# Fused attention and feed-forward: keys loaded straight with two heads side by side, three key and query buffers, values loaded later, key operands made in three portions

## The chip, the cores and the metric

The kernel runs on one core of a Trainium2 chip. The metric is the device time of one execution in microseconds; the profile gives the span from the first to the last instruction of one execution, and some time lies around it. The engines are named as in the profile: PE is TensorE (PEld its weight loads), DVE is VectorE, ACT is ScalarE, POOL is GpSimd, SP is SyncE, whose queue issues every DMA of this kernel.

## The reference

Block-compressed local attention over 2 batches of 8 heads (768 positions, 64 columns), then a feed-forward layer and a second one with a softmax-weighted norm. Cut to what matters:

```python
k_sum = k.reshape(B, H, nb, block, D).max(axis=3)      # block = 32
v_sum = v.reshape(B, H, nb, block, D).mean(axis=3)
scores_l = scale * (q @ k.T)                           # kept where |i - j| < 16
scores_s = scale * (q @ k_sum.T) + np.log(block)
a = softmax(concat([scores_l masked, scores_s]))
attn = a @ concat([v, v_sum])
x = attn heads side by side, 1536 x 512
h = x @ w_in;  y = (h * np.cos(h)) @ w_out             # 512 -> 2048 -> 512
h2 = y @ w_in2; solu = h2 * softmax(h2)                # 512 -> 1024
out = (layernorm(solu) * g_ln) @ w_out2                # 1024 -> 512
```

The weights come as 64-bit floats, read as pairs of 32-bit words.

## The kernel before

Attention comes first. Two heads make a pair (`n`, 0 to 7), and 4 tiles of 64 queries of a pair make a group (`G`, 0 to 23, three to a pair). A hand-written loop runs over `step` (0 to 28) and puts the stages of different groups behind each other: at a step, `emit_s` forms the scores of group step + 1 (`sps`), `emit_max` adds the mask and takes the row maximum of group step (VectorE, four instructions, then a subtraction on GpSimd), `emit_exp` takes the exponentials of group step - 1 (ScalarE), `emit_sum` and `emit_norm` the row sums (VectorE) and the normalisation (GpSimd) of group step - 2, `emit_t` and `emit_at` transpose the probabilities of group step - 4 on TensorE (`aps`) and copy them out (`at`, ScalarE, from group 20 on VectorE), and `emit_av` and `emit_x` form the products with the values of group step - 5 (`ops`) and copy them to `X`. Every engine takes its instructions in the order in which the code issues them.

Per pair, the keys and queries are loaded (`load_k`, `load_q`), copied so that the two heads lie side by side (`pair_k`, `pair_q`, tiles `kg` and `qg`), transposed on TensorE into the PSUM tile `qk` (`emit_k`, `emit_q`, at the step with g = 2, two pairs ahead), reduced to block maxima (`emit_ksum`, VectorE) and copied by ScalarE into the operands of the scores: `kx` in three instructions (inner windows, end windows, block maxima) and `qx`. The values are loaded in overlapping windows of 96 rows (`load_v`); `sum_v` sums them by blocks on TensorE, `scale_v` turns the sums into means on ScalarE (`vm`), and `place_vsum` writes the means with two DMAs into rows 96 to 119 of the value tile `vt`, from which the value products read them. `VSUM_AT` says at which step each pair's sums are formed; the means are placed one step later.

Beside this, the first eight weight tiles of the feed-forward are converted (`Weights`): `WSTEPS` lists the steps at which a tile is taken up (`bits`, which also issues the load of the next); ScalarE rescales its two words a step later, VectorE joins them (`s`), and the step after, ScalarE rounds the result (`w`) and GpSimd takes the difference. From step 15 on `fill` puts three or four products of the first feed-forward tiles (`h`) into each step. `warm_up` issues products of a zero tile.

SyncE's queue issues loads in the order of the code and stands still at an instruction whose buffer or semaphore is not free. By their shapes a load of keys or queries of a pair moves 384 KB, one of values 576 KB in four DMAs, a weight tile (`raw`) 512 KB, the means of a pair 144 KB in two DMAs, the mask 360 KB, the identity 64 KB.

From step 24 on the first feed-forward steps (`drain`) are mixed in; the feed-forward proper follows.

Of the kernel before, what the change touches and what calls it, by code (L numbers as in the profile page):

```python
# [18 lines left out]
BLOCK = 32  # L19
# [15 lines left out]
def fused_kernel(  # L35
# [58 lines left out]
    WSTEPS = (3, 6, 9, 12, 15, 18, 19, 20)  # L94
# [240 lines left out]
    def attention():  # L335
        st = ExitStack()
        with st:
# [27 lines left out]
            def load_k(n):  # L365
                k_t[n] = load_heads(k, n, "kt", 2)

            def side_by_side(t, name, scalar):
# [3 lines left out]
                if scalar:  # L372
                    nc.scalar.activation(out=to, in_=t, func=AF.Copy)
                else:
                    nc.vector.tensor_copy(to, t)
# [64 lines left out]
            def transposed(t, even, odd):  # L440

                for c in range(S // P):
                    nc.tensor.transpose(
                        (even, odd)[c % 2][:, (c // 2) * P:(c // 2 + 1) * P],
                        t[:, c].rearrange("p h d -> p (h d)"), ident)

            def emit_k(n):
                qk = ps_qk.tile([P, 2, 2, S // 2], F32, tag="qk", name="qk")
                transposed(k_t.pop(n), qk[:, 0, 0], qk[:, 0, 1])
                qk_t["k", n] = qk[:, 0]  # L450
                qk_t["q", n] = qk[:, 1, 0], qk[:, 1, 1]

            def emit_ksum(n):
                ksum = io.tile([P, NS], F32, tag="ksum", name="ksum")
                nc.vector.tensor_reduce(
                    out=ksum, in_=strided(qk_t["k", n], 0, [[BLOCK // 2, NS], [S // 2, 2], [1, BLOCK // 2]]),
                    op=ALU.max, axis=AX.XY)
                ks_t[n] = ksum

            def emit_kx(n):  # L460
                kps = qk_t.pop(("k", n))
                kx = io.tile([P, NT, KW], F32, tag="kx", name="kx")
                win = kx[:, :, 0:WIN].rearrange("p t (i r) -> p t r i", r=2)
# [8 lines left out]
                kx_t[n] = kx  # L472
# [10 lines left out]
            def emit_qx(n):  # L483
# [11 lines left out]
                kx_t[n] = (qx, kx_t[n])  # L495
# [3 lines left out]
            def emit_s(G):  # L499
                n, g = divmod(G, GPP)  # L500
                qx, kx = kx_t[n]
# [90 lines left out]
            warm_up(7)  # L592
            pair_k(0)
            emit_k(0)
            emit_ksum(0)
            pair_q(0)
            emit_q(0)
            emit_kx(0)
            emit_qx(0)
# [6 lines left out]
            VSUM_AT = {1: 0, 2: 1, **{3 * m - 2: m for m in range(2, NPAIR)}}  # L606
            for step in range(NGR + LA):
                n, g = divmod(step, GPP)
                summed = LN <= step < NGR + LN
                ahead = n + 1 if g == 0 and n + 1 < NPAIR else 0  # L610
# [4 lines left out]
                if step == 0:  # L615
                    emit_max(0)
                    pair_k(1)
# [19 lines left out]
                if ahead and step:  # L637
# [4 lines left out]
                if ahead and not step:  # L642
# [9 lines left out]
                if ahead:  # L652
                    emit_kx(ahead)
                    emit_qx(ahead)
# [7 lines left out]
                if g == 1 and n + 2 < NPAIR:  # L662
                    pair_k(n + 2)
# [5 lines left out]
                if g == 1 and n + 2 < NPAIR:  # L669
                    load_v(n + 2)  # L670
# [307 lines left out]
```

## Time and profile before

| | us |
|---|---|
| median of 3 runs | 492.09 (491.07 to 492.64) |
| the profiled execution: time | 493.62 |
| the profiled execution: span | 491.8 |
| TensorE busy (share of the span) | 477.3 (97%) |
| VectorE busy | 294.7 (60%) |
| ScalarE busy | 313.7 (64%) |
| GpSimd busy | 147.0 (30%) |

A busy TensorE is not one at its peak, and shares over the whole span are means over stages with different limits: attention takes the first fifth, where the transfers and all engines are in use, and the feed-forward the rest, in which TensorE hardly stops. The granted clock is 0.999 of full over the span.

### The profile page before, as it was taken

To read this page: it belongs to the slowest core of one execution; us is meant where nothing else is said; L and a number is where in the kernel's file an instruction comes from. 1 tells how busy PE (TensorE), PEld (TensorE's weight loads), DVE (VectorE), ACT (ScalarE), POOL (GpSimd) and SP (SyncE) were. 2 spreads that over 40 slices of the span, in tenths; PEclk is the share of its full clock that TensorE was granted. 3 is DMA by queue.
4 is the path that set the end of the run, shared out by engine and by line. 5 is a ranking of instruction groups with operands and counts; after the bars stand their busy time and mean duration, and the time that the engine had idled before them with its cause. 6 is when DMAs were issued, how large, how long until landed. Compare 5 with 4: busy or idle time off the path is not lost.

```text
span 491.8 us, 7868 instructions
## 1 busy us (share of the span) xinstructions
PE 477.3 (97%) x2938; PEld 391.7 (80%) x2938; DVE 294.7 (60%) x667; ACT 313.7 (64%) x540; POOL 147.0 (30%) x144
## 2 busy tenths in 40 slices
PE   7889999999999999999999999999999999999997
PEld 4677787678888888888888888888888888888886
DVE  3656775783445446556474655556477766776661
ACT  2568878756686666556655653788624867777621
POOL 1467887822432223222222220245500011110000
PEclk9999999999999999999999999999999999999999
DMA  7988964301222322232223220220001333224211
GB/s 206 239 222 221 258 146 110 110 2 39 91 85 85 116 99 87 87 123 92 85 90 119 92 85 23 93 100 1 0 1 43 87 86 86 66 64 65 68 39 44
DMA packets 59046, 46.17 MB, mean 94 GB/s; under 512 B 40448, under 2 KB 51328, under 8 KB 59008
## 3 DMA queue, kind: packets, MB, share of 16 engines
q1 hardware_dynamic: 59008, 45.67, 32.5%
q8 instruction: 23, 0.38, 0.3%
q14 instruction: 15, 0.12, 0.1%
HBM read 36.61 MB, written 3.15 MB: 81 GB/s over the span
## 4 chain that ended last, share of the span: by engine, by line
PE 84%; ACT 5%; DMA 3%; POOL 3%; issue 1%; SPq 1%; DVE 1%; ACTq 0%
PE y L276 27%; PE h L234 26%; PE o L853 13%; PE h L739 13%; DMA qt<-in_q_dram 2%; PE ops L562 1%; PE aps L544 1%; POOL sm L522 1%; PE sps L507 1%; ACT at L552 1%; DMA raw<-in_moe_w_in_dram 1%; ACT kx L464 1%; POOL w L187 1%; ACT sm L527 1%; SPq L393 1%
## 5 line engine op out<-in xcount | busy, mean ns | idle before, releaser
L234 PE MATMUL h<-xs,w 128*128 128x512 f32 x576 | 141.2, 391 | 0.0
L276 PE MATMUL y<-gs,w 128*128 128x512 f32 x576 | 138.2, 389 | 0.0
L276 PEld LDWEIGHTS y<-gs,w 128*128 128x128 f32 x576 | 108.0, 188 | 22.5
L234 PEld LDWEIGHTS h<-xs,w 128*128 128x128 f32 x576 | 107.2, 188 | 21.6
L187 POOL TENSOR_TENSOR w<-s,w 128x512 fp32r<-128x512 f32 x48 | 62.2, 1296 | 162.6 <-ACT w L186 139.6
L243 ACT ACTIVATE r<-h 128x512 int32<-128x512 f32 x48 | 28.6, 596 | 85.9 <-PE h L234 85.9
L248 DVE SCALAR_TENSOR_TENSOR r<-r,h 128x512 f32<-128x512 int32 x48 | 32.9, 685 | 67.2 <-ACT r L243 67.1
L171 DVE SCALAR_TENSOR_TENSOR s<-raw 128x512 int32<-128x512 int32 x48 | 35.8, 746 | 59.5 <-ACT raw L164 52.1
L853 PE MATMUL o<-w,ls 128*128 128x512 f32 (+1 forms) x312 | 67.8, 373 | 0.0
L739 PE MATMUL h<-w,xs 128*128 128x512 f32 x288 | 67.6, 390 | 0.0
L853 PEld LDWEIGHTS o<-w,ls 128*128 128x128 f32 x312 | 55.3, 188 | 10.7 <-DVE ls L829 0.4
L739 PEld LDWEIGHTS h<-w,xs 128*128 128x128 f32 x288 | 53.9, 188 | 11.2
L204 POOL TENSOR_TENSOR xs<-X,xs 128x512 fp32r<-128x512 f32 x22 | 30.6, 1397 | 39.1 <-ACT xs L203 39.1
L774 POOL TENSOR_TENSOR st<-st,mhalf 128x1 f32<-128x1 f32 x12 | 6.6, 550 | 110.1 <-DVE st L773 91.7
L253 ACT ACTIVATE r<-r,half_pi 128x512 f32<-128x512 f32 x48 | 34.4, 717 | 1.3 <-DVE r L248 1.3
L264 DVE TENSOR_TENSOR gs<-h,gs 128x512 fp32r<-128x512 f32 x48 | 32.6, 679 | 4.2 <-ACT gs L263 4.0
L163 ACT ACTIVATE raw<-raw 128x512 f32<-128x512 f32 x48 | 31.9, 664 | 2.0 <-DMA raw<-in_moe_w_in_dram 2.0
L258 DVE TENSOR_TENSOR h<-h,r 128x512 f32<-128x512 f32 x48 | 32.9, 684 | 0.4 <-ACT r L253 0.4
L164 ACT ACTIVATE raw<-raw 128x512 int32<-128x512 uint32 x48 | 31.9, 664 | 0.0
L186 ACT ACTIVATE w<-s 128x512 fp32r<-128x512 f32 x48 | 30.2, 629 | 1.5 <-DVE s L171 1.1
L756 ACT ACTIVATE e<-h,st 128x1024 f32<-128x1024 f32 (+1 forms) x13 | 13.6, 1048 | 26.4 <-DVE st L752 22.9
L522 POOL TENSOR_TENSOR sm<-sm,mx 128x480 f32<-128x480 f32 x24 | 24.1, 1006 | 17.6 <-DVE mx L518 17.5
(79 smaller groups left out, 553.9 us busy)
## 6 DMA issues: line engine op xcount, KB each, us to landing
raw<-in_moe_w_in_dram SPq DMA_DIRECT2D x24, 512.0 KB
raw<-in_moe_w_out_dram SPq DMA_DIRECT2D x24, 512.0 KB
vt<-in_v_dram SPq DMA_DIRECT2D x16, 240.0 KB
kt<-in_k_dram SPq DMA_DIRECT2D x8, 384.0 KB
qt<-in_q_dram SPq DMA_DIRECT2D x8, 384.0 KB
out_dram<-osb SPq DMA_DIRECT2D x11, 256.0 KB
vt<-vm SPq DMA_DIRECT2D x16, 72.0 KB
vt<-in_v_dram SPq DMA_DIRECT2D x16, 48.0 KB
```

The lines of the kernel that those rows point to most:

```text
L163: nc.scalar.activation(out=hw, in_=hw, func=AF.Prelu, scale=REBIAS, alpha=NEGATIVE)
L164: nc.scalar.activation(out=lw, in_=lw.bitcast(U32), func=AF.Copy, scale=TOP3)
L171: nc.vector.scalar_tensor_tensor(out=self.f32[i], in0=t[:, :, 1], scalar=3, in1=t[:, :, 0], op0=ALU.logical_shift_left, op1=ALU.bitwise_or)
L187: nc.gpsimd.tensor_tensor(out=w[:, 1, :], in0=f, in1=as32(w[:, 0, :]), op=ALU.subtract)
L234: nc.tensor.matmul(h, lhsT=w[:, a, f * P:(f + 1) * P], rhs=xs_of[tb, c][:, b_, :], start=(m == 0), stop=(m == 3 * KC - 1))
L248: nc.vector.scalar_tensor_tensor(out=r, in0=r.bitcast(I32), scalar=TWO_PI, in1=h_of[step], op0=ALU.mult, op1=ALU.subtract)
L253: nc.scalar.activation(out=r, in_=r, func=AF.Sin, scale=-1.0, bias=half_pi)
L258: nc.vector.tensor_tensor(out=h, in0=h, in1=r, op=ALU.mult)
L264: nc.vector.tensor_tensor(out=gs[:, 1, :], in0=r, in1=as32(gs[:, 0, :]), op=ALU.subtract)
L276: nc.tensor.matmul(y[e], lhsT=w[:, a, e * P:(e + 1) * P], rhs=gs[:, b_, :], start=(f == 0 and i == 0), stop=(f == GF - 1 and i == 2))
L739: nc.tensor.matmul(banks[n], lhsT=xs_of[NTB + t // TPB, c][:, a, t0:t0 + P], rhs=weights.done[w2i[c][n]][:, b_, :], start=(m == 0), stop=( ...
L853: nc.tensor.matmul(o, lhsT=ls_of[t][f // 4][:, a, s0:s0 + P], rhs=w[:, b_, cols], start=(f == 0 and i == 0), stop=(f == NF2 - 1 and i == 2))
```

## The change

Keys are loaded by two DMAs, one for each head, in pieces of 64 numbers, straight into the layout with two heads side by side; `pair_k` and the copy `kg` are gone. The transposed keys then stand in their natural order in PSUM, so that `ksum` and `kx` read them without a stride. Key and query tiles have three buffers instead of two. The first queries' copy moves from ScalarE to GpSimd. `kx` is split: the inner windows stay at the step with g = 0, the end windows and block maxima move to g = 1, and `qx` to g = 2 of the pair before. The first values are loaded after the keys and queries of pair 2, the others by a table `VLOAD_AT`; `VSUM_AT` forms the sums later, and `WSTEPS` takes the weight tiles up one step later. There are five more warm-up products.

```diff
-    WSTEPS = (3, 6, 9, 12, 15, 18, 19, 20)
+    WSTEPS = (4, 7, 10, 13, 16, 19, 20, 21)
...
-                t = io.tile([P, 2, NR, D], F32, tag=name, name=name)
+                t = io.tile([P, 2, NR, D], F32, tag=name, name=name, bufs=3)
...
             def load_k(n):
-                k_t[n] = load_heads(k, n, "kt", 2)
+                b, hp = divmod(n, NP)
+                t = k_t[n] = io.tile([P, NR, 2, D], F32, tag="kt", name="kt", bufs=3)
+                for j in range(2):
+                    nc.sync.dma_start(out=t[:, :, j, :], in_=k[b, 2 * hp + j].rearrange("(c p) d -> p c d", p=P))
...
-            def pair_k(n):
-                k_t[n] = side_by_side(k_t[n], "kg", False)
-
             def pair_q(n):
-                q_t[n] = side_by_side(q_t[n], "qg", n < 2)
+                q_t[n] = side_by_side(q_t[n], "qg", (nc.gpsimd, nc.scalar)[n] if n < 2 else nc.vector)
...
             def emit_k(n):
                 qk = ps_qk.tile([P, 2, 2, S // 2], F32, tag="qk", name="qk")
-                transposed(k_t.pop(n), qk[:, 0, 0], qk[:, 0, 1])
-                qk_t["k", n] = qk[:, 0]
+                t = k_t.pop(n)
+                kps = qk_t["k", n] = qk[:, 0].rearrange("p a s -> p (a s)")
+                for c in range(NR):
+                    nc.tensor.transpose(kps[:, c * P:(c + 1) * P], t[:, c].rearrange("p h d -> p (h d)"), ident)
...
             def emit_ksum(n):
                 nc.vector.tensor_reduce(
-                    out=ksum, in_=strided(qk_t["k", n], 0, [[BLOCK // 2, NS], [S // 2, 2], [1, BLOCK // 2]]),
-                    op=ALU.max, axis=AX.XY)
+                    out=ksum, in_=qk_t["k", n].rearrange("p (s b) -> p s b", b=BLOCK), op=ALU.max, axis=AX.X)
...
             def emit_kx(n):
                 nc.scalar.activation(
                     out=win[:, 1:NT - 1],
-                    in_=strided(kps, (QT - BAND) // 2, [[QT // 2, NT - 2], [S // 2, 2], [1, WIN // 2]]), func=AF.Copy)
+                    in_=strided(kps, QT - BAND, [[QT, NT - 2], [1, WIN]]), func=AF.Copy)
+
+            def emit_kx_ends(n):
+                kps, kx = qk_t.pop(("k", n)), kx_t["k", n]
+                win = kx[:, :, 0:WIN]
                 nc.scalar.activation(
                     out=win[:, 0:NT:NT - 1],
-                    in_=strided(kps, 0, [[(S - WIN) // 2, 2], [S // 2, 2], [1, WIN // 2]]), func=AF.Copy)
+                    in_=strided(kps, 0, [[S - WIN, 2], [1, WIN]]), func=AF.Copy)
                 nc.scalar.activation(
                     out=kx[:, :, WIN:KW], in_=ks_t.pop(n).unsqueeze(1).to_broadcast([P, NT, NS]), func=AF.Copy)
...
             load_k(1)
             load_q(1)
-            load_v(0)
             load_k(2)
             load_q(2)
-            load_v(1)
+            load_v(0)
...
-            VSUM_AT = {1: 0, 2: 1, **{3 * m - 2: m for m in range(2, NPAIR)}}
+            VSUM_AT = {3: 0, 4: 1, 7: 2, 9: 3, 12: 4, 13: 5, 16: 6, 19: 7}
+            VLOAD_AT = {1: 1, 4: 2, 6: 3, 8: 4, 10: 5, 13: 6, 16: 7}
...
+                if g == 1 and 0 < n < NPAIR - 1:
+                    emit_kx_ends(n + 1)
...
                 if ahead:
                     emit_kx(ahead)
-                    emit_qx(ahead)
+                if step == 1:
+                    emit_kx_ends(1)
+                if step == 0:
+                    emit_qx(1)
+                if g == 2 and n + 2 < NPAIR:
+                    emit_qx(n + 2)
...
                 if g == 1 and n + 2 < NPAIR:
-                    pair_k(n + 2)
                     pair_q(n + 2)
...
-                if g == 1 and n + 2 < NPAIR:
-                    load_v(n + 2)
+                if step in VLOAD_AT:
+                    load_v(VLOAD_AT[step])
```

How the order of instructions moves is shown at three places. First SyncE's queue at steps 2 to 4, where the block means `vm` of pairs 0 and 1 are written; a number behind a name tells buffers apart. Before, `vt_266` is the values of pair 2, `raw_319` and `raw_353` are weight tiles 0 and 1, `vt_121` the values of pair 0 and `kt_405` the keys of pair 4:

```order
L389 DMA vt_266<-in_v_dram 96x10x64
L393 DMA vt_266<-in_v_dram 96x2x64
L139 DMA raw_319<-in_moe_w_in_dram 128x1024
L436 DMA vt_121<-vm_271 12x12x128 x2
L139 DMA raw_353<-in_moe_w_in_dram 128x1024
L436 DMA vt_130<-vm_323 12x12x128 x2
L357 DMA kt_405<-in_k_dram 128x6x128
L357 DMA qt_407<-in_q_dram 128x2x384
```

Now `raw_292` and `raw_375` are weight tiles 0 and 1, `kt_380` the keys of pair 4, `vt_385` the values of pair 2 and `vt_128` those of pair 0:

```order
L139 DMA raw_292<-in_moe_w_in_dram 128x1024
L139 DMA raw_375<-in_moe_w_in_dram 128x1024
L369 DMA kt_380<-in_k_dram 128x6x64 x2
L357 DMA qt_383<-in_q_dram 128x2x384
L389 DMA vt_385<-in_v_dram 96x10x64
L393 DMA vt_385<-in_v_dram 96x2x64
L389 DMA vt_385<-in_v_dram 96x10x64
L393 DMA vt_385<-in_v_dram 96x2x64
L436 DMA vt_128<-vm_331 12x12x128 x2
L436 DMA vt_252<-vm_392 12x12x128 x2
```

The means of pair 0 were written right behind weight tile 0; now weight tile 1, the keys and queries of pair 4 and the values of pair 2 are issued ahead of them.

Second ScalarE at steps 5 and 6, from the exponentials of group 4 on (`sm4`). Before, with `X_75` the attention output and `kx_510`, `qx_514` the operands of pair 3:

```order
L527 ACTIVATE sm4_101<-sm4_101 128x4x120
L552 ACTIVATE at_465<-aps_425 120x512
L576 ACTIVATE X_75<-ops_443 128x256
L527 ACTIVATE sm5_102<-sm5_102 128x4x120
L552 ACTIVATE at_506<-aps_480 120x512
L576 ACTIVATE X_75<-ops_485 128x256
L464 ACTIVATE kx_510<-qk_430 128x10x2x48
L467 ACTIVATE kx_510<-qk_430 128x2x2x48
L470 ACTIVATE kx_510<-ksum_498 128x12x24
L493 ACTIVATE qx_514<-qk_430 128x768
```

Now, with `kx_493` and `qx_447` those of pair 3:

```order
L524 ACTIVATE sm4_101<-sm4_101 128x4x120
L163 ACTIVATE raw_292<-raw_292 128x512
L164 ACTIVATE raw_292<-raw_292 128x512
L549 ACTIVATE at_442<-aps_403 120x512
L573 ACTIVATE X_75<-ops_421 128x256
L490 ACTIVATE qx_447<-qk_408 128x768
L186 ACTIVATE w_474<-s_377 128x512
L524 ACTIVATE sm5_102<-sm5_102 128x4x120
L549 ACTIVATE at_489<-aps_460 120x512
L573 ACTIVATE X_75<-ops_465 128x256
L458 ACTIVATE kx_493<-qk_408 128x10x96
L524 ACTIVATE sm0_97<-sm0_97 128x4x120
```

`qx` of pair 3 moved up from behind `kx` to directly behind the first `X`, and weight tile 0 is now converted around it.

Third GpSimd near the end of attention; `sm2` to `sm5` are the groups 20 to 23 here, `sm0` and `sm1` the groups 18 and 19, L187 is a weight's difference, L522 (now L519) the subtraction of the maximum and L537 (now L534) the normalisation. Before:

```order
L187 TENSOR_TENSOR w_1314<-s_1223,w_1314 128x512
L522 TENSOR_TENSOR sm2_99<-sm2_99,mx_1323 128x4x120
L537 TENSOR_TENSOR sm0_97<-sm0_97,ss_1318 128x4x120
L187 TENSOR_TENSOR w_1364<-s_1279,w_1364 128x512
L522 TENSOR_TENSOR sm3_100<-sm3_100,mx_1373 128x4x120
L537 TENSOR_TENSOR sm1_98<-sm1_98,ss_1368 128x4x120
L187 TENSOR_TENSOR w_1411<-s_1334,w_1411 128x512
L522 TENSOR_TENSOR sm4_101<-sm4_101,mx_1418 128x4x120
L537 TENSOR_TENSOR sm2_99<-sm2_99,ss_1415 128x4x120
L522 TENSOR_TENSOR sm5_102<-sm5_102,mx_1451 128x4x120
```

Now:

```order
L519 TENSOR_TENSOR sm2_99<-sm2_99,mx_1312 128x4x120
L534 TENSOR_TENSOR sm0_97<-sm0_97,ss_1307 128x4x120
L187 TENSOR_TENSOR w_1355<-s_1271,w_1355 128x512
L519 TENSOR_TENSOR sm3_100<-sm3_100,mx_1364 128x4x120
L534 TENSOR_TENSOR sm1_98<-sm1_98,ss_1359 128x4x120
L187 TENSOR_TENSOR w_1403<-s_1325,w_1403 128x512
L519 TENSOR_TENSOR sm4_101<-sm4_101,mx_1412 128x4x120
L534 TENSOR_TENSOR sm2_99<-sm2_99,ss_1407 128x4x120
L187 TENSOR_TENSOR w_1442<-s_1375,w_1442 128x512
L519 TENSOR_TENSOR sm5_102<-sm5_102,mx_1449 128x4x120
```

Each of the last three weight differences moved behind one more group: the third stood ahead of the subtraction of group 22 and now stands ahead of that of group 23, the last.

## Rows read from the trace of the kernel before

**Rows 1.** Windows of 10 us: busy us (x instructions), granted clock, DMA share, GB/s.

```profile
core 0: us, PE busy (x) PEld busy (x) DVE busy (x) ACT busy (x) POOL busy (x), PEclk, DMA share, GB/s
0.00:10.00 10.00, 7.17 (x40) 3.90 (x42) 3.19 (x8) 3.59 (x5) 0.73 (x13) 1.00 0.79 230
10.00:20.00 10.00, 7.59 (x100) 6.24 (x96) 6.17 (x31) 4.30 (x8) 2.77 (x3) 1.00 0.80 206
20.00:30.00 10.00, 7.68 (x109) 6.53 (x110) 5.37 (x25) 6.30 (x13) 5.79 (x7) 1.00 0.88 232
30.00:40.00 10.00, 9.75 (x149) 8.17 (x148) 7.36 (x35) 8.31 (x19) 7.42 (x8) 1.00 0.91 236
```

**Rows 2.** Chain that ended last, 64 us on: start us, us, what.

```profile
66.17 0.70 PE h L234 x3
...
67.48 1.39 PE vsum L421 x24
68.88 0.97 PE sps L507 x16
69.84 0.58 PE aps L544 x4
70.43 0.76 PE qk L443 x6
...
103.97 5.69 PE y L276 x24
```

**Rows 3.** Windows of 1 to 3 us in the first 20 us.

```profile
11.00:14.00 3.00, 1.62 (x12) 1.27 (x12) 0.52 (x3) 0.84 (x1) 1.23 (x1) 1.00 0.27 62
14.00:15.00 1.00, 1.00 (x18) 0.81 (x17) 0.86 (x1) 0.00 (x0) 0.00 (x0) 1.00 1.12 325
17.00:18.00 1.00, 0.51 (x10) 0.51 (x12) 0.59 (x2) 1.00 (x4) 0.22 (x1) 1.00 1.19 259
18.00:19.00 1.00, 1.00 (x17) 0.84 (x12) 0.96 (x5) 0.58 (x2) 0.00 (x0) 1.00 0.47 118
```

**Rows 4.** Timeline of ScalarE, 12 to 18 us: start, us, instruction, [idle before <-releaser].

```profile
12.33 0.84 ACT L373 ACTIVATE qg<-qt 128x768 f32<-128x768 f32 x1 [3.60 <-DMA qt<-in_q_dram]
```

**Rows 5.** Timeline of TensorE, in four stretches between 17 and 98 us.

```profile
17.49 1.04 PE L507 MATMUL sps<-kx,qx 64*64 64x120 f32 x16 [0.96 <-ACT qx L493]
...
30.94 0.69 PE L562 MATMUL ops<-at,vt 120*64 120x64 f32 x16
...
33.95 1.04 PE L507 MATMUL sps<-kx,qx 64*64 64x120 f32 x16
...
48.81 0.62 PE L544 MATMUL aps<-ident,sm 128*120 128x128 f32 x4 [0.44 <-ACT at L552]
...
83.33 1.04 PE L507 MATMUL sps<-kx,qx 64*64 64x120 f32 x16
...
89.92 0.62 PE L544 MATMUL aps<-ident,sm 128*120 128x128 f32 x4 [0.28 <-ACT at L552]
...
92.44 0.62 PE L544 MATMUL aps<-ident,sm 128*120 128x128 f32 x4 [0.35 <-ACT at L552]
```

**Rows 6.** Timeline of GpSimd, 80 to 98 us.

```profile
81.75 1.29 POOL L187 TENSOR_TENSOR w<-s,w 128x512 fp32r<-128x512 f32 x1 [3.21 <-ACT w L186]
...
90.19 0.98 POOL L522 TENSOR_TENSOR sm<-sm,mx 128x480 f32<-128x480 f32 x1
...
92.08 0.98 POOL L522 TENSOR_TENSOR sm<-sm,mx 128x480 f32<-128x480 f32 x1
```

**Rows 7.** Groups by line, 0 to 130 us: busy us, mean ns | idle before.

```profile
L518 DVE CUSTOM_DVE_ANT_0 sm<-sps,mask 128x120 f32<-128x120 f32 x96 | 21.2, 278 | 0.8 <-PE sps L507 0.8
...
L455 DVE TENSOR_REDUCE ksum<-qk 128x24 f32<-128x768 f32 x8 | 7.5, 935 | 4.3 <-PE qk L479 2.6 <-PE qk L443 1.6
...
L576 ACT ACTIVATE X<-ops 128x256 f32<-128x256 f32 x19 | 7.3, 386 | 5.0 <-PE ops L562 5.0
...
L493 ACT ACTIVATE qx<-qk 128x768 f32<-128x768 f32 x7 | 5.8, 823 | 0.0
```

More of the change, by code (lines that the diff above doesn't have):

```diff
@@ L455, in emit_ksum @@
                 nc.vector.tensor_reduce(
-                    out=ksum, in_=strided(qk_t["k", n], 0, [[BLOCK // 2, NS], [S // 2, 2], [1, BLOCK // 2]]),
-                    op=ALU.max, axis=AX.XY)
+                    out=ksum, in_=qk_t["k", n].rearrange("p (s b) -> p s b", b=BLOCK), op=ALU.max, axis=AX.X)
                 ks_t[n] = ksum
             def emit_kx(n):
-                kps = qk_t.pop(("k", n))
-                kx = io.tile([P, NT, KW], F32, tag="kx", name="kx")
-                win = kx[:, :, 0:WIN].rearrange("p t (i r) -> p t r i", r=2)
+                kps = qk_t["k", n]
+                kx = kx_t["k", n] = io.tile([P, NT, KW], F32, tag="kx", name="kx")
+                win = kx[:, :, 0:WIN]
                 nc.scalar.activation(
                     out=win[:, 1:NT - 1],
-                    in_=strided(kps, (QT - BAND) // 2, [[QT // 2, NT - 2], [S // 2, 2], [1, WIN // 2]]), func=AF.Copy)
+                    in_=strided(kps, QT - BAND, [[QT, NT - 2], [1, WIN]]), func=AF.Copy)
+            def emit_kx_ends(n):
+                kps, kx = qk_t.pop(("k", n)), kx_t["k", n]
+                win = kx[:, :, 0:WIN]
                 nc.scalar.activation(
                     out=win[:, 0:NT:NT - 1],
-                    in_=strided(kps, 0, [[(S - WIN) // 2, 2], [S // 2, 2], [1, WIN // 2]]), func=AF.Copy)
+                    in_=strided(kps, 0, [[S - WIN, 2], [1, WIN]]), func=AF.Copy)
                 nc.scalar.activation(
                     out=kx[:, :, WIN:KW], in_=ks_t.pop(n).unsqueeze(1).to_broadcast([P, NT, NS]), func=AF.Copy)
-                kx_t[n] = kx
             def emit_q(n):
@@ L494, in emit_qx @@
                         out=rows, in_=strided(src[0], 0, [[1, P], [P, NR]]), func=AF.Copy, scale=0.125)
-                kx_t[n] = (qx, kx_t[n])
+                kx_t["q", n] = qx
             sm_t, at_t, ss_t, o_t, sum_t = {}, {}, {}, {}, {}
@@ L500, in emit_s @@
                 n, g = divmod(G, GPP)
-                qx, kx = kx_t[n]
+                qx, kx = kx_t["q", n], kx_t["k", n]
                 sps = bank(G % 2, "sps").rearrange("p (i s) -> p i s", i=NG)[:, :, 0:KW]
@@ L585, in attention @@
             load_q(1)
-            load_v(0)
             load_k(2)
             load_q(2)
-            load_v(1)
+            load_v(0)
             nc.gpsimd.memset(small, 0.0)
             nc.gpsimd.memset(strip, 0.0)
-            warm_up(7)
-            pair_k(0)
+            warm_up(8)
             emit_k(0)
@@ L596, in attention @@
             pair_q(0)
+            warm_up(4)
             emit_q(0)
             emit_kx(0)
+            emit_kx_ends(0)
             emit_qx(0)
@@ L609, in attention @@
                 summed = LN <= step < NGR + LN
-                ahead = n + 1 if g == 0 and n + 1 < NPAIR else 0
+                ahead = 1 if step == 1 else n + 1 if g == 0 and 0 < n < NPAIR - 1 else 0
                 warm_up(IDLE[g] if step < min(FILL) else 0)
@@ L616, in attention @@
                     emit_max(0)
-                    pair_k(1)
                     pair_q(1)
@@ L634, in attention @@
                     emit_exp(step - LX)
+                if g == 1 and 0 < n < NPAIR - 1:
+                    emit_kx_ends(n + 1)
                 if summed:
                     emit_sum(step - LN)
-                if ahead and step:
+                if ahead and step > 1:
                     emit_ksum(ahead)
@@ L641, in attention @@
                     emit_max(step)
-                if ahead and not step:
+                if step == 1:
                     emit_ksum(ahead)
@@ L653, in attention @@
                     emit_kx(ahead)
-                    emit_qx(ahead)
+                if step == 1:
+                    emit_kx_ends(1)
[3 more added lines that the diff above has]
+                    emit_qx(n + 2)
                 if step == 2:
```

11 lines of the change are left out of this document (3 added, 8 removed).

## The prediction

> **What bounds it now.** I read the windows of ten microseconds first [rows 1]. TensorE is busy 7.2, 7.6 and 7.7 us of the first three tens and 9.75 of the fourth, so its idle time lies in the first 30 us. Then the chain that ended last: from 103.97 us on it is TensorE's feed-forward products [rows 2], which the diff leaves as they are. So the change can act only on the 104 us of attention, and there on three stretches with different limits.
>
> Until about 31 us the transfers set the pace: the DMA engines are busy 79, 80 and 88% and move 230, 206 and 232 GB/s [rows 1]. In narrower windows the reader sees two holes, 62 GB/s over 11 to 14 us and 118 over 18 to 19 us, beside stretches of 325 and 259 [rows 3]. ScalarE sits 3.60 us until pair 1's queries have landed and starts the copy `qg` at 12.33 [rows 4]; the first scores of pair 1 start at 17.49 [rows 5].
>
> From 34 to 80 us TensorE is the bound. The chain there is its own pieces one behind the other: `h` products 0.70 us, value sums 1.39, scores 0.97, probability transposes 0.58, key transposes 0.76 [rows 2]. What is left to gain are single waits: 0.44 us for ScalarE's `at` at 48.81 [rows 5], and two more of about half a microsecond, for ScalarE too, at 59 and 79 us.
>
> From 81 us GpSimd holds the chain: three rounds of weight difference, subtraction and normalisation back to back; the 3.21 us ahead of the first `w` is its last idle time for ten [rows 6].
>
> **The key loads.** A load stays 384 KB (by the code's shapes, as all sizes here), but its pieces shrink from 512 to 256 bytes. The values always came in pieces of 256: 17 to 18 us, nearly all of it values, ran at 259 GB/s; 14 to 15 us, keys in pieces of 512, at 325 [rows 3]. I take 255 against 305, both a little under these best windows: 393 kB / 255 = 1.54 us against 1.29, so **+0.25 us a load**; the bounds are 0 (the pieces are not what limits) and +0.62 (206 GB/s, the slowest ten microseconds [rows 1]: 1.91 against 1.29). The Trainium skill, "DMA: Bandwidth & Descriptors", section Specifications, asks for at least 512 bytes for line rate, since smaller pieces are read, modified and written; it speaks against this change. The trace agrees that pieces of 256 are slower, by a fifth [rows 3].
>
> **The copies.** `kg` is gone from VectorE. VectorE was busy at most 7.4 of 10 us up to 40 [rows 1], and the key transposes wait for loads; I cost the copy's loss at zero, bounds 0 and -0.5 (one copy ahead of the first transposes). GpSimd's copy of the first queries is new there: between 0.8 us (ScalarE's copy, 0.84 [rows 4]) and twice that. It delays pair 0's scores by up to a microsecond, hidden behind pair 1's queries, which land no earlier than before: two key loads stand ahead of them, so their copy starts at about 12.8. From that copy to pair 1's scores it took 17.49 - 12.33 = 5.2 us; the links are the same operations in another order (`ksum` now behind `qx`), so about 18.0. Without that cover the microsecond would count. The five extra warm-up products run in idle time.
>
> **The order of loads: pair 0's block means come late.** The first value products `ops` need these means written into `vt`. Their write stood behind raw tile 0 in SyncE's queue; now raw 1, keys and queries 4 and values 2 stand ahead too. Up to it the queue moves 5 x 384 (keys) + 5 x 384 (queries) + 3 x 576 (values) + 2 x 512 (raw) + 424 (identity, mask) = 7,016 KB, with the means 7.33 MB. At the old pace, 6.68 MB by 30 us and then 236 GB/s [rows 1], that is 30 + 0.65/0.236 = 32.75 us. Two corrections. The holes close, because with a third buffer SyncE issues on without waiting for a copy: 11 to 14 us moved 186 kB where 265 GB/s, the pace beside the holes with room to spare, would have given 795, and 18 to 19 lost 147 in the same way: together 756 kB or 2.85 us. Five key loads cost 5 x 0.25 = 1.25. **Landing at 31.2 us**; bounds 29.9 (no cost of the pieces) and 35.9 (the holes stay, +0.62 a load).
>
> TensorE gets to these products at 18.0 plus its work in the new order: four scores groups 3.9, two value sums 2.8, two probability transposes 1.2, two sets of key and query transposes 3.0 (queries as keys), some 0.8 of waits for the maxima: 29.7 us. So it waits 1.5 us and starts them at 31.2; before it was 30.94 [rows 5].
>
> What stands behind them: on ScalarE that group's `X`, then directly pair 3's `qx`, a weight and the exponentials; on VectorE pair 3's `ksum`, which waits for `qx`, and the maxima behind it; and the scores of group 8 need the bank that those maxima free. From the start of the value products: 0.69 [rows 5], then `X` 0.39, `qx` 0.82, `ksum` 0.94, four maxima of 0.28 [rows 7] = 3.9 us. Scores of group 8 at 35.1 instead of 33.95 [rows 5]: **+1.15 us**.
>
> **One value sum later.** Before, three value sums had run by then; now two. The third still comes: **+1.4** [rows 2].
>
> **ScalarE evened out.** `kx`, its ends and `qx` no longer come in one burst, so the three waits near 49, 59 and 79 us lose their cause, 1.4 together, and some small ones with them: -1.8. In return the chain `X`, `qx`, `ksum`, maxima, 3.3 us, now stands in TensorE's way at steps 9, 12, 15 and 18: covered by scores, transposes, value products and a value sum at 9 and 12 (3.6 us), not quite by three `h` products in the sum's place at 15 and 18 (2.9): 0.3 to 0.4 each. Net **-1.2**, bounds -1.8 and -0.5.
>
> **Weights one step later.** GpSimd's three rounds start with the scores of group 22 (83.33 [rows 5]) instead of 21. The first weight difference stood 1.5 us behind its step's scores; one small ScalarE copy less is ahead of it now, so 1.1: at 84.4. From it to the third subtraction behind it took 90.19 - 81.75 = 8.44 us [rows 6]; that is now the last group's, at 92.9 instead of 92.08 [rows 6]. Behind it wait the last exponentials, a table load and the first feed-forward steps, which VectorE has ahead of the `at` that frees the bank of the next transposes. **+0.8**, bounds 0 and 1.2.
>
> **Sum.** 1.15 + 1.4 - 1.2 + 0.8 = +2.15. The profiled execution took 493.62 us, 491.8 of it span, so 495.8 in one like it; it lies 1.53 above the median of the runs shown, 492.09, and against that median the forecast is **494.2 us**.
>
> **Rivals.**
> 1. *The means land in time (not slower).* If the transfers run at 300 GB/s once SyncE is never stopped, 7.33 MB are through by 27 us. Then TensorE's arrival at 29.7 decides, group 8 starts at 33.6, and the sum is -0.35 + 1.4 - 1.2 + 0.8 = +0.65: 492.7 us. It decides from a landing before 29.7. For it: the 325 GB/s window; against it: no ten microseconds of the first forty gave over 236.
> 2. *Faster.* Pair 1's queries landed late because value pieces were on the DMA engines beside them. With the values behind, they come at 10.5, 1.8 earlier, and the means with them at 29.4 (group 8 at 33.3, -0.65); the middle's waits all go (-1.8); and with TensorE ahead the old waits of 0.28 and 0.35 for `at` at 89.92 and 92.44 [rows 5] go too and cover the shift of the rounds: -0.65 + 1.4 - 1.8 - 0.6 = -1.65: 490.4. Against it: the queue serves its loads in order, and other loads take the place of those values.
> 3. *Small pieces cost double.* Each key load +1.29 instead of +0.25: the means land at 31.2 + 5 x 1.04 = 36.4, and the sum is 7.35: 499.4. The values' 259 GB/s speak against it.
>
> **How the numbers follow.** About 0.3% (1.5 us) is what a measurement of this kernel can tell from no change. Chances: the forecast 0.40, rival 1 0.30, rival 2 0.23, rival 3 0.07. The forecast's own range is 492.3 (the means at 29.9, the middle -1.8) to 497 (the means at 33.9, half way to their bound). The range that holds 8 in 10 takes in rival 1 and rival 2 and leaves out rival 3: 489.8 to 497. Faster by over 0.3%: 0.23. Slower: 0.42, the forecast but for its low edge, and rival 3. Within: 0.35.
>
> **What would show it.** In the profile after: no hole in the transfers at 11 to 14 us; the means' DMA as releaser of the first `ops`, near 31 us; group 8's scores after 35; no TensorE waits for `at` or `qx` between 45 and 80; the last subtraction on GpSimd later against TensorE's scores. If the first `ops` starts before 30 us, if pair 1's queries land by 11, or if the middle still loses more than 2 us, the forecast is wrong.

## The result and the profile after

The changed kernel takes 494.98 us (median of 10 runs, 493.82 to 496.83), the one before 492.04 (10 runs, 490.11 to 493.52): 1.0068 of it, with a 95% interval of 1.0052 to 1.0083. It is slower by 2.9 us. The profiled execution took 495.19 us, 493.4 of it span; the granted clock is 0.993 of full over the span.

First the windows of the changed kernel that answer to [rows 1] and [rows 3] (start and end, length, busy time of PE, PEld, DVE, ACT and POOL with counts, granted clock, DMA share, GB/s):

```profile
10.00:20.00 10.00, 7.52 (x78) 6.49 (x76) 5.50 (x30) 4.33 (x8) 3.86 (x4) 0.83 1.05 250
...
30.00:40.00 10.00, 7.80 (x114) 6.53 (x114) 5.81 (x29) 6.08 (x13) 5.31 (x5) 0.83 0.92 211
...
11.00:14.00 3.00, 2.21 (x28) 1.81 (x26) 1.60 (x10) 1.55 (x3) 1.91 (x2) 1.00 1.07 272
...
28.00:30.00 2.00, 0.52 (x5) 0.28 (x3) 1.83 (x3) 0.10 (x1) 0.54 (x1) 1.00 0.28 55
```

From 11 to 14 us there is no hole, 272 GB/s instead of 62 [rows 3], and the second ten moves 250 GB/s instead of 206 [rows 1]; whether the change did that is taken up with the second profile of before, below. TensorE is busy only 7.80 us of the fourth ten instead of 9.75, from 28 to 30 us the transfers nearly stop (55 GB/s), and twice the granted clock falls, to 0.83 as the mean of ten microseconds.

The chain that ended last, across that place (start, duration, what):

```profile
25.79 2.32 SPq L393
...
28.21 1.00 SPq L436
...
29.26 2.89 DMA vt<-vm
...
32.20 0.69 PE ops L559 x16
```

SyncE issues the last values of pair 2 up to 28.1 us, only then the means of pair 0 (line 436); 2.89 us later they have landed, and the first value products start at 32.20. Now the timeline of the changed kernel at the places of [rows 4 to 6]:

```profile
10.40 0.84 ACT L376 ACTIVATE qg<-qt 128x768 f32<-128x768 f32 x1 [1.63 <-DMA qt<-in_q_dram]
...
15.69 1.86 PE L504 MATMUL sps<-kx,qx 64*64 64x120 f32 x16 [2.48 <-ACT kx L468]
...
22.53 0.27 ACT L429 ACTIVATE vm<-vsum 128x128 f32<-128x128 f32 x1
...
32.20 0.69 PE L559 MATMUL ops<-at,vt 120*64 120x64 f32 x16 [3.68 <-DMA vt<-vm]
32.81 1.86 PE L504 MATMUL sps<-kx,qx 64*64 64x120 f32 x16
...
36.49 1.04 PE L504 MATMUL sps<-kx,qx 64*64 64x120 f32 x16
...
84.09 1.04 PE L504 MATMUL sps<-kx,qx 64*64 64x120 f32 x16
...
105.45 5.73 PE L276 MATMUL y<-gs,w 128*128 128x512 f32 x24
```

Pair 1's queries are copied at 10.40 instead of 12.33 [rows 4], and pair 1's scores start at 15.69 instead of 17.49 [rows 5], but at half the granted clock (0.50 over 16 to 19 us): 1.86 us for a group instead of 1.04. The means were ready on ScalarE at 22.8 us; TensorE then waits 3.68 us for their write, and the scores behind it take 1.86 us again. Group 8 (36.49) is 2.54 us behind [rows 5], group 22 (84.09) 0.76, the feed-forward 1.55 behind 103.90, its start in the timeline (the chain of [rows 2] dates it 0.07 later). From group 8 to 90 us TensorE's timeline shows no wait at all; the waits of before at 48.81, 59 and 79 us are gone.

The profiled execution before lay 1.5 us above its median, so the kernel before was profiled once more (below, 492.02 us). By stages, in us, each number the start of the first matmul of its kind in the timeline:

| | first `ops` | scores 8 | scores 22 | first `y` | 8 to 22 | 22 to `y` |
|---|---|---|---|---|---|---|
| before, first profile | 30.94 | 33.95 | 83.33 | 103.90 | 49.38 | 20.57 |
| before, second | 29.30 | 32.30 | 81.70 | 102.29 | 49.40 | 20.59 |
| after | 32.20 | 36.49 | 84.09 | 105.45 | 47.60 | 21.36 |

Against the second profile the front costs 4.19 us, the middle gives back 1.80, the end costs 0.77: +3.16, close to the medians' 2.94.

### The profile page after: what moved, and what is told of

Read it like the earlier page. It is cut to its first block, busy times and chain, and to the rows that moved or that the text cites. A ratio compares the mean times of both kernels' runs of the same rounds, so it can differ in the third digit from the quotient of the medians.

```text
span 493.4 us, 7884 instructions
## 1 busy us (share of the span) xinstructions
PE 478.9 (97%) x2943; PEld 393.9 (80%) x2943; DVE 295.1 (60%) x659; ACT 313.3 (63%) x539; POOL 149.6 (30%) x145
## 4 chain that ended last, share of the span: by engine, by line
PE 90%; ACT 2%; SPq 2%; DVE 2%; POOL 2%; DMA 1%; issue 1%
PE y L276 27%; PE h L234 25%; PE o L856 13%; PE h L742 13%; PE sps L504 3%; PE ops L559 2%; PE aps L541 2%; PE vsum L421 2%; PE qk L445 1%; PE qk L476 1%; DMA qt<-in_q_dram 1%; SPq L393 1%; ACT qx L490 1%; POOL sm L519 1%; PE tp L790 1%
## 5 line engine op out<-in xcount | busy, mean ns | idle before, releaser
L187 POOL TENSOR_TENSOR w<-s,w 128x512 fp32r<-128x512 f32 x48 | 62.1, 1293 | 169.0 <-ACT w L186 146.0
L171 DVE SCALAR_TENSOR_TENSOR s<-raw 128x512 int32<-128x512 int32 x48 | 37.3, 777 | 51.1 <-ACT raw L164 44.5
L204 POOL TENSOR_TENSOR xs<-X,xs 128x512 fp32r<-128x512 f32 x22 | 29.6, 1351 | 32.9 <-ACT xs L203 32.9
L504 PE MATMUL sps<-kx,qx 64*64 64x120 f32 x384 | 26.3, 280 | 3.3 <-ACT kx L468 2.5
```

The source lines that it names most:

```text
L171: nc.vector.scalar_tensor_tensor(out=self.f32[i], in0=t[:, :, 1], scalar=3, in1=t[:, :, 0], op0=ALU.logical_shift_left, op1=ALU.bitwise_or)
L187: nc.gpsimd.tensor_tensor(out=w[:, 1, :], in0=f, in1=as32(w[:, 0, :]), op=ALU.subtract)
L504: nc.tensor.matmul(sps[h, i, :], lhsT=qx[h, t * QT:(t + 1) * QT], rhs=kx[h, t, :], start=True, stop=True)
```

## The experiments

**Before, once more.** No edit.

> The kernel before once more, for a second profile of it. Its first profile took 493.62 us, 1.5 more than its median, so part of what the two first profiles show as equal may be chance. If the difference lies in the first loads, the scores of pair 0 start earlier than 9.07 us here and the feed-forward products before 103.97; if it lies elsewhere, another stretch is shorter.

It took 492.02 us. A window of it, and timeline rows of TensorE:

```profile
11.00:14.00 3.00, 2.25 (x35) 2.05 (x32) 1.37 (x9) 0.84 (x1) 1.24 (x1) 1.00 0.85 253
```

```profile
29.30 0.69 PE L562 MATMUL ops<-at,vt 120*64 120x64 f32 x16
...
32.30 1.04 PE L507 MATMUL sps<-kx,qx 64*64 64x120 f32 x16 [0.15 <-DVE mx L518]
...
81.70 1.04 PE L507 MATMUL sps<-kx,qx 64*64 64x120 f32 x16
...
102.29 5.76 PE L276 MATMUL y<-gs,w 128*128 128x512 f32 x24
```

Pair 0's scores started later here (9.98 against 9.07 us), so the very first loads were not the difference. The loads behind them were: the same kernel, still with two buffers, moves 253 GB/s over 11 to 14 us where its first profile shows 62 [rows 3], and 275 instead of 206 in the second ten [rows 1]; pair 1's queries are copied at 11.13 instead of 12.33 [rows 4]. Missing are the two waits that the first profile had at 25.11 us (1.15, for pair 2's values) and at 28.86 (1.16, for `at`; 0.49 here). From group 8 on the two profiles agree to 0.02 us in each stage.

So the hole at 11 to 14 us comes and goes in one and the same kernel, and with it a wait for values. That the third buffer closed it is not shown (a version with three buffers, the one with the values as before, has a hole of 61 GB/s at 18 to 19 us), and against this profile the queries come only 0.7 us earlier in the changed kernel.

**Theory A, the order in SyncE's queue.** Edit to the changed kernel:

```diff
-            VLOAD_AT = {1: 1, 4: 2, 6: 3, ...
+            VLOAD_AT = {1: 1, 5: 2, 6: 3, ...
```

> The changed kernel with the values of pair 2 loaded one step later, so that in SyncE's queue the means of pair 0 stand ahead of them instead of behind. Theory A (the loss is the late write of pair 0's means: in the changed kernel the means are made on ScalarE at 22.8 us but SyncE, busy with the four value loads ahead, issues their write only at 28.2, and the first value products wait 3.68 us for it and then run at half the granted clock): SyncE reaches the write near 22.8 us, the first value products start when TensorE arrives, at 28.5, no half clock behind them; 4 to 5 us less than the changed kernel's 494.98, that is about 490.5. Theory B (the queue is simply full, it matters little which 144 KB go first): the wait shrinks by less than 1 us and the time stays at 494 or above.

491.53 us, 0.9991 of before (0.998 to 1.0001): the loss is gone with one number of the table. SyncE's and TensorE's rows:

```profile
21.88 2.52 SPq L436 DMA_DIRECT2D vt<-vm  x2
...
29.03 0.69 PE L559 MATMUL ops<-at,vt 120*64 120x64 f32 x16 [1.67 <-DMA vt<-vm]
...
32.69 1.04 PE L504 MATMUL sps<-kx,qx 64*64 64x120 f32 x16 [0.81 <-DVE mx L515]
```

SyncE issues the means at 21.88 us instead of 28.21; the wait is 1.67, the granted clock is 1.00 in every ten microseconds, and group 8 comes at 32.69, 3.8 us sooner. Theory B falls; theory A has the cause, but not the whole size, since 1.67 us of the wait are left. The small pieces of the keys are all still there, so what this edit won back is not their price.

Then the second weight tile was put behind the means as well:

```diff
-                if step in WSTEPS:
+                if step in WSTEPS and step != 4:
                     weights.bits()
...
                     place_vsum(VSUM_AT[step - 1])
+                if step == 4:
+                    weights.bits()
```

> The changed kernel with the values of pair 2 loaded one step later and, besides, the second weight tile's load put behind the means of pair 0 at step 4. With the values alone moved, SyncE issued the means at 21.9 us, but they landed at 28.9, behind 512 KB each of two weight tiles and 768 KB of keys and queries; TensorE waited 1.67 us. Theory A (what counts is how many bytes stand ahead in the queue): 512 KB at 250 GB/s are 2.1 us, the wait goes: 489.9 us. If the write's own time decides (two DMAs of many small pieces), the wait stays and so do 491.5 us.

491.18 us, 0.9981 (0.9964 to 0.9998). TensorE and SyncE:

```profile
17.43 1.04 PE L504 MATMUL sps<-kx,qx 64*64 64x120 f32 x16 [2.48 <-ACT kx L468]
...
22.96 1.84 SPq L436 DMA_DIRECT2D vt<-vm  x2
...
28.59 0.69 PE L559 MATMUL ops<-at,vt 120*64 120x64 f32 x16
...
32.26 1.04 PE L504 MATMUL sps<-kx,qx 64*64 64x120 f32 x16 [0.82 <-DVE mx L515]
```

The means are issued before the weight tile, no wait is left at 28.59. The wait shown went as theory A says; in the time it is 0.1%, which the intervals do not part. This is the only one of twelve intervals that lies below 1, and its upper end is 0.9998: weak evidence of a gain.

**Values later, alone, in the kernel before.** The changed kernel's tables `VSUM_AT` and `VLOAD_AT` and its order of the first loads, nothing else.

> The kernel before with one part alone: values loaded and summed later (the changed kernel's order and tables), all else as before, two buffers and keys in pieces of 512 bytes with their copy. Theory A (late means alone lose the time): TensorE waits 3 us or more ahead of the first value products, for the means; 495 to 496 us. Rival (it takes the smaller pieces of the keys or the third buffer as well to make them late): a wait under 1.5 us and 492 to 493.

493.41 us, 1.002 (0.9997 to 1.0042). Theory A in this form was wrong:

```profile
18.74 1.86 PE L507 MATMUL sps<-kx,qx 64*64 64x120 f32 x16 [2.38 <-ACT qx L493]
...
27.07 3.54 SPq L436 DMA_DIRECT2D vt<-vm  x4
...
31.14 0.69 PE L562 MATMUL ops<-at,vt 120*64 120x64 f32 x16
```

The means are issued nearly as late, at 27.07, but nobody waits for them: pair 1's scores start at 18.74, and TensorE comes to the first value products at 31.14 by itself. Here the late write costs nothing, because TensorE is late too. The rival's size came out nearly, not its reason: the means were late without smaller pieces and without a third buffer.

**Values as before, in the changed kernel.** The old tables and the old order of the first loads.

> The changed kernel with the values loaded and summed where the kernel before has them (values 0 ahead of the keys of pair 2, values 1 behind its queries, then one pair ahead at every step with g = 1; sums at steps 1, 2, 4, 7 and so on). The straight keys, three buffers, the evened ScalarE and the later weights stay. Theory A (only the late means lose time): the first value products start at 31 us or earlier, the middle keeps its gain of 1.8 to 3.1 us, the tail its loss of 0.8, so 490 to 491 us. Rival (the values were put later because their pieces hold up pair 1's queries): the queries land after 12 us again, pair 1's scores start after 17, and 492 to 493.

495.44 us, 1.0054 (1.0025 to 1.0083): against both expectations. TensorE's waits:

```profile
16.07 1.04 PE L504 MATMUL sps<-kx,qx 64*64 64x120 f32 x16 [1.02 <-ACT kx L468]
...
24.87 1.62 PE L421 MATMUL vsum<-vt,strip 96*64 96x128 f32 x24 [1.48 <-DMA vt<-in_v_dram]
...
37.01 2.92 PE L421 MATMUL vsum<-vt,strip 96*64 96x128 f32 x24 [1.82 <-DMA vt<-in_v_dram]
...
56.67 1.04 PE L504 MATMUL sps<-kx,qx 64*64 64x120 f32 x16 [0.82 <-DVE mx L515]
```

Pair 1's scores start at 16.07, and its queries are copied at 10.59, with the values ahead as before, so value pieces do not hold up the queries: the rival falls. There is no wait for the means. Instead the value sums come before their values (1.48 us at step 4, 1.82 at step 7, that one then at half clock, 2.92 us for the sum), and the maxima are late by 0.82 us three times (one shown). The old sum steps were too early for a TensorE that is ahead, and they leave the chain `X`, `qx`, `ksum`, maxima without cover at steps 9 and 12. From group 8 to 22 it takes 51.74 us instead of the changed kernel's 47.60. So, in the changed kernel, the later values were needed; what lost time was the means' place among them.

**The evened ScalarE, alone, in the kernel before.** `emit_kx_ends` and `emit_qx` moved as in the change, the strided key order kept.

> The kernel before with one part alone: the key operand made in three portions and the query operand a step earlier (inner windows at g = 0, ends and maxima at g = 1, queries at g = 2 of the pair before); pair 1 stays in one burst at step 0. The forecast's term: -1.2 us net (-1.8 for the waits, +0.6 for the chain at steps 15 and 18), 490.6 us; the stretch from the scores of group 8 to those of group 21 from 46.27 to about 45. The trace of the changed kernel suggests more, -3 us: 489 us, that stretch 43.3. If the gain there came from TensorE being late with its whole work behind it, nothing: 491.8.

495.54 us, 1.0052 (1.0034 to 1.007): slower, against every expectation. VectorE, GpSimd and TensorE:

```profile
38.78 0.54 DVE L375 COPY kg<-kt 128x768 f32<-128x768 f32 x1
39.25 1.63 DVE L375 COPY qg<-qt 128x768 f32<-128x768 f32 x1
...
39.15 1.31 POOL L204 TENSOR_TENSOR xs<-X,xs 128x512 fp32r<-128x512 f32 x1 [0.84 <-ACT xs L203]
...
40.94 0.87 PE L482 MATMUL qk<-ident,qg 128*128 128x128 f32 x6 [0.68 <-DVE qg L375]
...
45.41 1.04 PE L510 MATMUL sps<-kx,qx 64*64 64x120 f32 x16 [0.62 <-DVE mx L521]
```

The same two instructions in the first profile of before, VectorE and GpSimd:

```profile
39.13 0.55 DVE L375 COPY qg<-qt 128x768 f32<-128x768 f32 x1
...
39.37 1.45 POOL L204 TENSOR_TENSOR xs<-X,xs 128x512 fp32r<-128x512 f32 x1 [1.51 <-ACT xs L203]
```

At the steps with g = 1 VectorE copies keys and queries, `kg` and `qg`, and three times TensorE waits 0.68 us for the second; the chain `X`, `qx`, `ksum`, maxima makes the scores of a later step wait 0.62 twice and 0.26 once. From group 8 to 22 it takes 51.25 us instead of 49.40; the rest of the loss lies in the front, where group 8 comes at 34.39 instead of 32.30, and is not explained here.

The wait for `qg` comes less from `kg`, which takes no longer than before, than from `qg` itself: 1.63 us instead of 0.55. In three slow cases (39.25, 50.26, 61.26) GpSimd had begun `xs` 0.1 us earlier, and the copy ended about 0.4 us behind it; in the fourth (72.29) the copy began ahead of `xs`, as at 39.13 in before, and took 0.55. So a small shift in who starts first costs a microsecond. No run moved `xs` by itself, so this is read from the rows and not tested.

In the changed kernel TensorE shows neither wait: `kg` is gone, `qg` takes 0.95 us, and the sums at steps 9 and 12 stand where TensorE would wait. Evening out alone lost time as it fell out here; with the other parts the middle takes 47.60.

**Straight keys, alone, in the kernel before.** Two DMAs a pair, natural order, no `kg`; two buffers.

> The kernel before with one part of the change alone: keys loaded straight by two DMAs a pair in pieces of 256 bytes, no copy that pairs them, natural order in PSUM; two buffers, the old order of loads, ScalarE and weights as before. The forecast's price of 0.25 us a load gives at most 5 x 0.25 = 1.25 us on the write of pair 0's means, and a little back for the copy: 492.0 to 493.3 us. The rival that small pieces cost double says 5 us more, about 497. If the copy of the keys was what held the pace of the loads (two buffers freed late), faster: 490 to 491.5.

493.35 us, 1.0026 (1.0009 to 1.0043), 0.4 to 2.1 us more. TensorE in the front:

```profile
24.36 1.62 PE L421 MATMUL vsum<-vt,strip 96*64 96x128 f32 x24 [1.19 <-DMA vt<-in_v_dram]
...
28.77 0.63 PE L545 MATMUL aps<-ident,sm 128*120 128x128 f32 x4 [1.82 <-ACT at L553]
...
34.56 1.04 PE L508 MATMUL sps<-kx,qx 64*64 64x120 f32 x16 [0.74 <-DVE mx L519]
```

The middle gains 0.65 us (48.75), group 8 comes at 34.56, with the two waits that the first profile of before had too. A price of five times 0.25 us lies within the interval, nothing and double both lie outside; that it is the pieces and not those chance waits is argued, not shown, and what the missing copy gives back in the middle is in the sum too. The Trainium skill, "DMA: Bandwidth & Descriptors", Specifications, asks for 512 bytes or more; the time agrees with it in sign.

**The waits filled.** `warm_up(8)` ahead of the scores of step 2, `warm_up(12)` ahead of the value products of step 5.

> The changed kernel with products of a zero tile put into TensorE's two long waits: 8 ahead of the first scores of pair 1 (about 2.1 us of a wait of 2.48) and 12 ahead of the first value products (about 3.1 us of 3.68). The waits themselves stay. Theory A2 (a part of the loss is the granted clock, at half after each of these waits, and it fell because TensorE stood idle): the granted clock stays near 1.0 from 10 to 20 and 30 to 40 us; the pieces behind the second wait run at the speed of before, 1.5 us less: 493.4 us; what is saved behind the first wait is lost in the second, which the means end. If the clock falls for another reason or its cost is hidden: 495 us.

495.23 us, 1.0066 (1.0047 to 1.0086). A window and TensorE's rows:

```profile
10.00:20.00 10.00, 9.20 (x99) 6.69 (x97) 6.45 (x34) 4.16 (x7) 3.73 (x4) 1.00 0.97 239
```

```profile
33.91 0.69 PE L559 MATMUL ops<-at,vt 120*64 120x64 f32 x16 [2.40 <-DMA vt<-vm]
34.53 1.86 PE L504 MATMUL sps<-kx,qx 64*64 64x120 f32 x16
```

With the first wait filled the granted clock stays at 1.00 from 10 to 20 us (0.83 in the changed kernel); that the filling did it is not shown, since it stays at 1.00 there in the two repaired kernels above with the wait unfilled. Behind the second, the idle products ended 2.40 us before the means, and the clock fell all the same. From pair 0's scores to group 8 it took 27.27 us (10.93 to 38.20) against 27.57: nothing won, because the means end the front. The price of the clock can't be read from this run.

**Weights as before.** First all eight steps of `WSTEPS` back, in the changed kernel:

> The changed kernel with the weight tiles taken up at the steps of the kernel before. The forecast's term of +0.8 us for weights one step later: 494.2 us, with the last subtraction on GpSimd 0.8 us earlier against the last scores. If GpSimd's rounds do not hold the chain at the end of attention, no change from 494.98. If ScalarE is what the earlier weights disturb, slower.

495.84 us, 1.0069 (1.0044 to 1.0094), no gain. TensorE:

```profile
85.49 1.04 PE L504 MATMUL sps<-kx,qx 64*64 64x120 f32 x16
...
106.21 5.73 PE L276 MATMUL y<-gs,w 128*128 128x512 f32 x24
```

From group 22 to the feed-forward 20.72 us instead of 21.36: 0.64 of the end's 0.77 is the weights' place, as forecast. But 8 to 22 takes 48.60 instead of 47.60. Then only the last three, beside the two edits of theory A:

```diff
-    WSTEPS = (4, 7, 10, 13, 16, 19, 20, 21)
+    WSTEPS = (4, 7, 10, 13, 16, 18, 19, 20)
```

> The changed kernel with values of pair 2 one step later, the second weight tile behind the means (491.18 us so far), and the last three weight tiles taken up at steps 18, 19 and 20 again, as before, instead of 19, 20 and 21; the five ahead stay. Theory (the later rounds of GpSimd cost the end 0.8 us, as forecast; with all eight tiles moved back the stretch from group 21's scores to the first feed-forward products fell from 24.46 to 23.82 us): 0.65 us less, 490.5. Rival (what is saved at the end is lost at steps 18 to 20 in the middle): 491.2.

490.70 us, 0.9984 (0.9963 to 1.0005). The end takes 20.74 us instead of 21.36, the middle 48.07 instead of 47.59: of 0.62 won 0.48 is lost again. The rival holds: this is no different from 491.18.

**Pair 1's chain.** TensorE waits 2.48 us ahead of pair 1's scores in the changed kernel and its repairs. First its operand at step 0, beside the two edits of theory A:

```diff
-                ahead = 1 if step == 1 else n + 1 if g == 0 and 0 < n < NPAIR - 1 else 0
+                ahead = n + 1 if g == 0 and n < NPAIR - 1 else 0
...
-                if step == 1:
+                if step == 0:
                     emit_ksum(ahead)
...
-                if step == 1:
+                if step == 0:
                     emit_kx_ends(1)
```

> The changed kernel with values of pair 2 one step later, the second weight tile behind the means (491.18 us so far), and besides pair 1's block maxima and key operand made at step 0 again, as in the kernel before, instead of step 1. There TensorE waits 2.48 us ahead of pair 1's first scores, for the last portion of the key operand, which stands behind the maxima and exponentials of the groups before. Theory (that order alone holds it): the wait shrinks to about 1 us, 1.5 us less in the end, 489.7. Rival (the front is bound by transfers again: the means of pair 0 land when they land): the time goes into a wait for the means or for values, 491.

491.60 us, 0.9994 (0.9974 to 1.0013): no gain, and the theory of the order falls. VectorE, ScalarE, TensorE:

```profile
12.82 0.96 DVE L450 TENSOR_REDUCE ksum<-qk 128x24 f32<-128x768 f32 x1 [1.38 <-PE qk L476]
...
13.81 0.97 ACT L458 ACTIVATE kx<-qk 128x960 f32<-128x960 f32 x1 [3.12 <-DVE ksum L450]
...
15.22 0.81 ACT L490 ACTIVATE qx<-qk 128x768 f32<-128x768 f32 x1
...
16.09 1.04 PE L504 MATMUL sps<-kx,qx 64*64 64x120 f32 x16 [2.33 <-ACT qx L490]
```

The wait is 2.33: block maxima, keys and queries still follow one another, in another order. All three read one PSUM tile. The Trainium skill, "PSUM — Partial Sum Buffer", section PSUM bank collisions raise a hardware error, says that two engines may not touch one bank at once, reads included; the rows agree in that `ksum` on VectorE and the copies on ScalarE don't overlap. The last run took the queries out of that tile. Besides, it has pair 1's operand at step 0, the two edits of theory A, the last three weight tiles as before, and the means of pair 0 ahead of pair 4's loads; the diff shows only the edit for the queries:

```diff
-                if n == 0:
+                if n < 2:
                     qk_t["q", n] = bank(2, "q0"), bank(3, "q1")
...
-                if n == 0:
+                if n < 2:
                     for r in range(2):
```

> The changed kernel with all that helped: values of pair 2 one step later, the second weight tile behind the means, the last three weight tiles as before (490.70 us so far). Besides, pair 1's queries are transposed into PSUM tiles of their own and scaled on VectorE, and its key operand is made at step 0; and the means of pair 0 stand ahead of the keys and queries of pair 4 in SyncE's queue. In the run with pair 1 at step 0 alone, block maxima (0.96 us), three portions of keys (0.97, 0.33, 0.44) and queries (0.81) ran one behind the other, since all read one PSUM tile, and TensorE waited 2.33 us. Theory (the wait is that chain): the queries drop out of it, the wait falls to about 1.2 us and the end comes 1.2 us earlier, 489.5. Rival (the transfers take it back, as a wait for means or values): 490.7 or more.

491.73 us, 0.9988 (0.9972 to 1.0005). VectorE, ScalarE, TensorE:

```profile
13.12 1.01 DVE L486 TENSOR_SCALAR qx<-q 128x384 f32<-128x384 f32 x2
...
13.24 0.97 ACT L458 ACTIVATE kx<-qk 128x960 f32<-128x960 f32 x1 [2.18 <-DVE ksum L450]
...
15.09 1.04 PE L504 MATMUL sps<-kx,qx 64*64 64x120 f32 x16 [1.25 <-DVE mx L515]
...
32.51 1.60 PE L421 MATMUL vsum<-vt,strip 96*64 96x128 f32 x24 [0.35 <-DMA vt<-in_v_dram]
...
53.37 1.62 PE L421 MATMUL vsum<-vt,strip 96*64 96x128 f32 x24 [0.54 <-ACT X L573]
```

Queries and keys now overlap (13.12 and 13.24), the wait is 1.25, group 8 comes at 29.92, 2.5 us sooner than in the run with the last weights moved (32.40). But 8 to 22 takes 49.54 instead of 48.07, with new waits of 0.35 us for pair 2's values and 0.54 for ScalarE's `X` among others, and the medians show no gain. The profiled execution is the fastest of the twelve (489.91 us), so its rows flatter this version. The rival holds.

## Why the prediction was right

The forecast, 494.2 us, slower, came out at 494.98. The place and the cause of the loss were right. That the number came so near is in part luck: by stages, and against the second profile of before, the front lost 3.04 us more than forecast and the middle came out 2.00 better, so that the errors partly cancel (+3.16 in all against a forecast of +2.15).

- **Place and mechanism of the loss: right, and shown.** Pair 0's means late behind the new loads, as releaser of the first `ops`. One entry of a table takes the loss away.
- **Size of the front, +1.15 forecast, +4.19 measured.** Three terms make the difference. The base: in the second profile of before group 8 comes 1.65 us sooner than in the one the sum was made against. The landing: 32.2 instead of 31.2. The way from the first `ops` to group 8: 4.29 us instead of 3.9; with nearly the same order and the clock at full it took 3.66 (29.03 to 32.69), so the half clock cost some 0.63 there. 1.15 + 1.0 + 0.39 + 1.65 = 4.19.
- **The landing came near by two errors.** The sum took bytes by pace, the means last, 0.6 us for their 147 kB. The transfers were faster: 7.13 MB had moved by 28 us (2.31 and 2.50 in the first two tens, 2.32 in the next 8 us), and nearly all that stood ahead was through. But SyncE was still issuing the last values of pair 2 up to 28.1 us, the last of them for 2.32 us, and from the start of its issue the write of the means took 3.9 us, to 32.15, while the transfers fell to 55 GB/s (28 to 30 us). What set the landing was when SyncE issued the write, and the write's own time, not the pace of the bytes.
- **The holes: not shown.** The 2.85 us taken off for them rest on a hole that the second profile of the same kernel does not have.
- **TensorE's arrival: wrong, without effect on the time.** "Pair 1's queries land no earlier than before" failed: their copy started at 10.40, not 12.8, and TensorE stood at 28.5, not 29.7. As the landing set the start, this made the wait longer (3.68 us instead of 1.5) and not the kernel. By the prediction's own sign (queries landed by 11) its account of this stretch was wrong.
- **The middle, +1.4 for a third sum and -1.2 for the evened ScalarE forecast, -1.80 measured.** The third sum did move into it, so evening out, the missing copy with the straight order, and the later sums together gave 3.2 us, not 1.2. The bounds of -1.8 to -0.5 took evening out as one part with its own price; alone the stretch was 1.9 us longer.
- **The copies at zero: wrong in the middle.** The reason given was VectorE's slack up to 40 us. With the keys straight and `kg` gone the middle alone gains 0.65 us. GpSimd's copy of the first queries took 0.82 us, the lower end of what was forecast.
- **The end, +0.8: right,** 0.77.
- **Small pieces:** +1.25 in all is within what the keys alone cost; rival 3 (499.4) falls. Rival 2 (490.4) had its premise come true, the queries at 10.4, but not its reason: with the values ahead as before they came at 10.59. The early queries made TensorE early and the means no earlier. Rival 1's pace of 300 GB/s did not come over ten microseconds, 231 to 250 in each of the first three tens; from 20 to 26 us it did, 311 to 337, and the means were late all the same.

## What to carry to other kernels

A write that an engine waits for has a place in a queue, and its price is the wait of whoever needs it: find who issues it, what that engine issues ahead of it, and when the needer will arrive after the change, not before it. Gains ahead of such a write are lost in it until it is moved too. Parts of a change that fill each other's waits have no prices of their own: with evening out alone the middle was 1.9 us longer, with its partners it gained 1.8 and took up a third sum. Where a profile's own time lies above the median, profile again before making a sum on its stages: the hole that this prediction closed was not there the second time.

## What the runs showed of the hardware

TensorE's granted clock fell to half (0.50, 1.2 of 2.4 GHz) behind single idle stretches: of 2.48 us and 3.68 us in the changed kernel, of 2.40 us with the rest of the wait filled. It need not: behind the same 2.48 us it stayed at 1.00 from 10 to 20 us in two of the repaired kernels and fell to 0.85 in a third. The kernel before shows 1.00 there in its first profile [rows 1] and 0.95 in its second.

The copy `qg` on VectorE took 0.55 us when it began ahead of GpSimd's `xs` and 1.63 when it began 0.1 us behind it. SyncE's issue of one and the same 48 KB value load took 0.56 to 0.57 us in seven of 16 cases in the changed kernel and up to 2.37 in the others.
